# Four-head loads, the first batch's norm on VectorE, and v in token order in a Nystrom attention with two MLPs

## The chip, the core and the metric

The kernel runs on one core of a Trainium2 chip. The metric is the device time of one execution in microseconds (us); less is better. A NeuronCore has five engines that run side by side, each with its own instruction stream in a fixed order: TensorE (PE in the profile; its weight loads are PEld), VectorE (DVE), ScalarE (ACT), GpSimd (POOL) and SyncE (SP). Transfers between memory and the on-chip SBUF are issued by SP or ACT onto a queue and carried by 16 DMA engines.

## The reference

The input is q, k and v of 4 batches, 8 heads, 576 tokens and 64 channels. Per head the tokens are cut into 32 segments of 18, and a landmark is the mean of a segment. Then two MLPs run over the 2304 tokens of 512 channels.

```
q_lm, k_lm = segment means (32 landmarks of 18 tokens each)
A  = softmax(q  k_lm^T / 8)        # 576 x 32
Bm = softmax(q_lm k_lm^T / 8)      # 32 x 32
C  = softmax(q_lm k^T / 8)         # 32 x 576
Z  = Bm^T / (norm1 * norminf);  six times: Z = 2 Z - Z Bm Z
x  = A Z C v                       # heads side by side: 512 channels
x  = x / rms(x) * g;  x = (silu(x w_gate) * (x w_val)) w_out     # 512 -> 1536 -> 512
out = (s * relu(x w_in)^2 + b) w_out2                            # 512 -> 2048 -> 512
```

The MLP weights arrive as 64-bit floats and are narrowed to 32 bits on the chip.

## The kernel before

The kernel does not write its instructions down in the order in which they run. Every step is an entry in a list (`op`, and `at` inside `attention`) with the engines that may do it and an assumed duration on each, the buffers that it reads and writes, and a key. `Scheduler.run` plays the list through with those durations and emits an instruction when the planned clock reaches it, the smallest key first; so the order on every engine, and which engine does a step that has two, come from the plan. On the chip each engine then goes through its stream in that order and waits where a result is missing.

`attention(b, ...)` is one batch. Batches 2 and 3 are "fine" (`FINE = 2`), batches 0 and 1 are not; the change treats these two kinds differently. The steps of a batch: load q, k (two tiles each, `load_heads`, four heads of 32 landmarks on the 128 partitions of a tile) and v (`load_v`); sum the segments (`seg_sum`: in batch 0 a reduction on VectorE, in the others five adds per tile on GpSimd, L488 to L493); transpose q and k on TensorE (L528) with evictions on ScalarE (L532); the 32 x 32 scores Bm; the two halves of C (`c_side`: scores, maximum, exponential at L687, transposes at L704, product with v at L726); the four pieces of A (`a_side`); six Newton steps for Z (products at L586, updates at L631 on VectorE), after which `w_bd` (L790) forms Z C v; the product with A and its squares (L828, L834); the sum of squares over channels and the root (L848 to L859); a diagonal of the roots (L861), its product with ones on TensorE (L866) that spreads the root over partitions, the scaling (L872), and the split of x into two rounded parts (L876 and L878). That last part, from L834 on, is called the norm here.

The first MLP begins with `fused` (L993), which multiplies the norm's weights into w_gate and w_val, and `hidden`, whose matrix products stand at L1016 and whose element-wise steps at L1032 (tanh on ScalarE), L1034 and L1038. A batch has 12 such units of two halves, and `out_mm` follows. The first L1016 is where batch 0 of the MLP starts. The weights of the first MLP are loaded and narrowed while batch 0 runs: `narrow` loads 512 KB of 64-bit words into one of three `stage` buffers (L904 or L906, on SP) and needs four element-wise steps (L917 and L919 on ScalarE, L921 and L924 on VectorE, which reads two SBUF operands in both); the result is stored in device memory (L937, L949) and read again for batches 1 to 3. Where the plan leaves TensorE idle in the first 60 us, `warm` (L1248) puts products of ones there whose result nobody reads.

A load's order in time is its place in SP's stream; a load that must wait (for its buffer, or for the eighth DMA before it, since the DMAs share eight semaphores) holds all that stands behind it on SP.

Of the kernel before, what the change touches and what calls it, by code (L numbers as in the profile page):

```python
# [35 lines left out]
SCORE = 0.56  # L36
# [213 lines left out]
def tile_nystrom_attention_two_mlps(  # L250
# [150 lines left out]
    def attention(b, t0, t1):  # L401
# [17 lines left out]

        pair = xs[1, b] = (Buf(x_r[0]), Buf(x_r[1]))  # L420
# [130 lines left out]
        def b_mm(_):  # L551
            for g in range(2):
                if not fine:
                    for h in range(4):
                        p = slice(32 * h, 32 * h + 32)
                        nc.tensor.matmul(
                            out=pB.t[p, 32 * g:32 * g + 32], lhsT=bd["q", g].t[0:D, p],
                            rhs=bd["k", g].t[0:D, p], start=True, stop=True)
# [83 lines left out]
        def scores(ps, nm, g, hf, p0, r, w):  # L642
            d, t = bd["kq"[nm == "k"], g], tt[nm, g]
# [12 lines left out]
            def mm(_):  # L656
                for h in range(4):
                    p = slice(32 * h, 32 * h + 32)
                    e = slice(D * hf, D * hf + D)
                    nc.tensor.matmul(  # L660
                        out=ps.t[p, 0:HC], lhsT=d.t[e, p],
                        rhs=t.t[e].rearrange("p (t m) -> p t m", m=128)[:, :, p], start=True, stop=True)

            at(("pe", SCORE), p0 + 0.02, mm, r=[d, *[(t, i) for i in range(3)], *r], w=[ps, *w])
# [4 lines left out]
        def c_side(g, p0):  # L669
            transposed("k", g, p0)  # L670
# [15 lines left out]
            for hf in range(2):  # L686
                at(("act", t_act(HC) + 0.19), p0 + 0.03, lambda e, hf=hf: e.activation(  # L687
                    out=eC.t[:, HC * hf:HC * hf + HC], in_=pC[hf].t[:, 0:HC], func=ACTF.Exp,
                    scale=scale, bias=cm.t[:, 3:4], accum_out=cs.t[:, hf:hf + 1]),
                    r=[pC[hf], (cm, 3)], w=[(eC, hf), (cs, hf)])  # L690
# [19 lines left out]
            at(("pe", 0.13), p0 + 0.04, lambda e: tr(e, [4]), r=[(eC, 1), "ident", (pE[1], "taken")], w=[pE[1]])  # L710
# [29 lines left out]
        def a_side(hf, g, p0):  # L740
            if hf == 0:
                transposed("q", g, p0)
# [72 lines left out]
        for hf in range(2):  # L815
# [21 lines left out]
            if not first:  # L837
                for c, n in ((2, 2 * HC), (1, HC)):
                    at(dp(n), p0 + 0.03, lambda e, c=c, n=n, xq=xq: e.tensor_tensor(
                        out=xq.t[:, 0:n], in0=xq.t[:, 0:n], in1=xq.t[:, HC * c:HC * c + n], op=ALU.add),  # L840
                        r=[(xq, i) for i in range(KD)] if n > HC else [(xq, 0), (xq, c)],
                        w=[(xq, 0)] + ([(xq, 1)] if n > HC else []))
            n_sum = KD if first else 1
# [10 lines left out]
            def s_rec(e, pS=pS, rs=rs):  # L854
# [5 lines left out]
                out=rs.t[0:NP, 0:3], in_=rs.t[0:NP, 0:3], func=ACTF.Sqrt), r=[rs, "table"], w=[rs])  # L860
            at(dp(HC), p0 + 0.07, lambda e, rs=rs, dg=dg: e.tensor_tensor(  # L861
# [3 lines left out]
                op=ALU.mult), r=[rs, "ident"], w=[dg])  # L865
# [3 lines left out]
            for g in range(2):  # L869
# [8 lines left out]
                at(dp(HC), p0 + 0.1, lambda e, a=a, cols=cols: e.tensor_tensor(  # L878
                    out=part(1, "t")[:, cols], in0=a.t[:, 0:HC], in1=part(0, "t")[:, cols].bitcast(F32),
                    op=ALU.subtract), r=[a, wh[0]], w=wl)  # L880
# [103 lines left out]
    def fused(key, b, f):  # L984
# [12 lines left out]
        op(("pe", U_PE), key, mm, r=[gw[b], (r, 0), (r, 1)], w=[*pU, (uh, "taken"), (ul, "taken")])  # L997
# [287 lines left out]
```

## Time and profile before

| | |
|---|---|
| median of 3 runs | 906.83 us (901.38 to 908.39) |
| the profiled execution, its own time | 903.9 us |
| its span, first to last instruction | 902.2 us |
| TensorE busy | 870.2 us, 96% of the span |
| VectorE, ScalarE, GpSimd busy | 700.9, 430.0, 114.4 us |
| mean granted TensorE clock | 0.987 of full speed |
| moved by DMA | 105.99 MB, mean 117 GB/s |

The share of TensorE says little by itself: it holds the warm products of the first 60 us, and from 170 us on it is close to 99%. What differs between stages is what TensorE waits for, so the rows below are taken from stretches of the span.

### The profile page before, as it was taken

To read this page: it belongs to the slowest core of one execution; us is meant where nothing else is said; L and a number is where in the kernel's file an instruction comes from. 1 tells how busy PE (TensorE), PEld (TensorE's weight loads), DVE (VectorE), ACT (ScalarE), POOL (GpSimd) and SP (SyncE) were. 2 spreads that over 40 slices of the span, in tenths; PEclk is the share of its full clock that TensorE was granted. 3 is DMA by queue.
4 is the path that set the end of the run, shared out by engine and by line. 5 is a ranking of instruction groups with operands and counts; after the bars stand their busy time and mean duration, and the time that the engine had idled before them with its cause. 6 is when DMAs were issued, how large, how long until landed. Compare 5 with 4: busy or idle time off the path is not lost.

```text
span 902.2 us, 17055 instructions
## 1 busy us (share of the span) xinstructions
PE 870.2 (96%) x6453; PEld 726.4 (81%) x6453; DVE 700.9 (78%) x1486; ACT 430.0 (48%) x902; POOL 114.4 (13%) x152
## 2 busy tenths in 40 slices
PE   8897899899999999999999999999999999999997
PEld 5576666798788898899888988888888888888896
DVE  5768889889888889799889866676667666666686
ACT  3565566535465345555656533343343334333453
POOL 0442034500465004300000000000000000000000
PEclk9898999999999999999999999999999999999999
DMA  7778998886444432348887200010001000100100
GB/s 162 198 214 283 247 280 236 271 241 216 119 144 141 143 116 84 106 146 272 286 262 252 56 1 1 0 47 1 1 1 47 1 1 1 47 1 1 27 22 24
DMA packets 72899, 105.99 MB, mean 117 GB/s; under 512 B 25968, under 2 KB 46448, under 8 KB 72816
## 3 DMA queue, kind: packets, MB, share of 16 engines
q1 hardware_dynamic: 72240, 103.45, 38.3%
q10 hardware_dynamic: 576, 1.44, 0.7%
q8 instruction: 51, 0.84, 0.4%
q14 instruction: 32, 0.26, 0.1%
HBM read 90.70 MB, written 14.16 MB: 116 GB/s over the span
## 4 chain that ended last, share of the span: by engine, by line
PE 83%; DVE 8%; DMA 5%; ACT 2%; issue 1%; SPq 1%; ACTq 0%; DVEq 0%
PE bank L975 22%; PE bank L1091 22%; PE bank L1016 15%; PE bank L1065 12%; PE bank L1061 3%; PE bank L993 3%; DMA region<-in_q_dram 2%; DVE cmag L921 2%; DMA stage<-in_moe_w_out_dram 2%; PE bank L648 1%; PE bank L828 1%; DMA stage<-in_moe_w_gate_dram 1%; PE bank L1248 1%; DVE wl L893 1%; DVE rawg L924 1%
## 5 line engine op out<-in xcount | busy, mean ns | idle before, releaser
L1016 PE MATMUL bank<-xh,uh 128*128 128x288 f32 x384 | 124.2, 323 | 6.4 <-DVE hbuf L1034 3.1
L975 PE MATMUL bank<-xh,ul 128*128 128x512 f32 (+1 forms) x320 | 117.7, 368 | 0.0
L975 PE MATMUL bank<-xh,uh 128*128 128x512 f32 (+1 forms) x320 | 117.6, 368 | 0.0
L975 PE MATMUL bank<-xl,uh 128*128 128x512 f32 (+1 forms) x320 | 117.6, 368 | 0.0
L1016 PE MATMUL bank<-xl,uh 128*128 128x288 f32 x384 | 114.8, 299 | 0.0
L1016 PE MATMUL bank<-xh,ul 128*128 128x288 f32 x384 | 114.7, 299 | 0.0
L1091 PE MATMUL bank<-wh,hh 128*128 128x512 f32 x288 | 112.4, 390 | 0.3 <-DVE hh L892 0.3
L1091 PE MATMUL bank<-wl,hh 128*128 128x512 f32 x288 | 112.3, 390 | 0.0
L1226 ACT ACTIVATE hbuf<-bank 128x512 f32<-128x512 f32 (+1 forms) x79 | 43.9, 556 | 143.4 <-PE bank L975 143.3
L1091 PE MATMUL bank<-wh,hl 128*128 128x512 f32 x288 | 112.0, 389 | 0.0
L1016 PEld LDWEIGHTS bank<-xh,uh 128*128 128x128 f32 x384 | 73.6, 192 | 27.3 <-issue 5.0
L1065 PE MATMUL bank<-hh,wh 128*128 128x288 f32 x288 | 87.9, 305 | 1.1 <-ACT xbuf L1075 1.1
L1065 PE MATMUL bank<-hl,wh 128*128 128x288 f32 x288 | 84.9, 295 | 0.1
L1065 PE MATMUL bank<-hh,wl 128*128 128x288 f32 x288 | 84.6, 294 | 0.0
L893 DVE TENSOR_TENSOR hl<-hbuf,hh 128x512 fp32r<-128x512 f32 (+2 forms) x123 | 73.1, 595 | 2.3
L1016 PEld LDWEIGHTS bank<-xl,uh 128*128 128x128 f32 x384 | 73.7, 192 | 0.5
L1016 PEld LDWEIGHTS bank<-xh,ul 128*128 128x128 f32 x384 | 73.7, 192 | 0.0
L975 PEld LDWEIGHTS bank<-xh,uh 128*128 128x128 f32 x320 | 60.2, 188 | 11.1
L975 PEld LDWEIGHTS bank<-xl,uh 128*128 128x128 f32 x320 | 60.0, 188 | 10.9
L975 PEld LDWEIGHTS bank<-xh,ul 128*128 128x128 f32 x320 | 60.1, 188 | 10.2
L917 ACT ACTIVATE ca<-stage 128x512 f32<-128x512 f32 x68 | 45.9, 675 | 42.6 <-DMA stage<-in_moe_w_out_dram 12.0
L892 DVE CAST uh<-region 128x512 fp32r<-128x512 f32 x56 | 23.9, 426 | 54.4 <-PE bank L975 54.4
(193 smaller groups left out, 1822.9 us busy)
## 6 DMA issues: line engine op xcount, KB each, us to landing
rawo<-kepto SPq DMA_DIRECT2D x84, 256.0 KB, 3.3
rawg<-keptg SPq DMA_DIRECT2D x36, 512.0 KB, 3.9
stage<-in_moe_w_out_dram SPq DMA_DIRECT2D x28, 512.0 KB, 5.2
stage<-in_moe_w_in_dram SPq DMA_DIRECT2D x16, 512.0 KB, 4.6
stage<-in_moe_w_gate_dram SPq DMA_DIRECT2D x12, 512.0 KB, 5.3
stage<-in_moe_w_val_dram SPq DMA_DIRECT2D x12, 512.0 KB, 5.5
keptg<-rawg SPq DMA_DIRECT2D x12, 512.0 KB, 6.3
region<-in_k_dram SPq DMA_DIRECT2D x32, 144.0 KB, 5.3
```

Of the source, the lines that this page charges most:

```text
L648: nc.tensor.matmul(out=ps.t[:, 0:HC], lhsT=part(u, "bd")[:, 128 * e:128 * e + 128], rhs=part(y, "t").rearrange("p (t e i) -> p t e i", e=2 ...
L892: else e.tensor_copy(out=hi(), in_=src())), r=r, w=[wh], pair=True)
L893: b = op({"dve": t_dve(n), "pool": t_pool(n)}, key, lambda e: e.tensor_tensor(out=lo(), in0=src(), in1=hi().bitcast(F32), op=ALU.subtract) ...
L917: op(("act", 0.08 + t_act(512)), key, lambda e: e.activation(out=a.t, in_=word(1).bitcast(F32), func=ACTF.Copy, scale=2.0 ** -112), r=[st, ...
L921: op(("dve", t_dve(512)), key, lambda e: e.scalar_tensor_tensor(out=m.t, in0=word(1), scalar=-2 ** 31, in1=m.t, op0=ALU.bitwise_and, op1=A ...
L975: nc.tensor.matmul(out=ps.t[:, 0:n], lhsT=w[a].t[:, ks], rhs=x[y].t[:, kd, 0:n], start=(kd == 0 and i == 0), stop=(kd == KD - 1 and i == 2))
L993: nc.tensor.matmul(out=pU[g].t[m, 0:256], lhsT=gw[b].t[p, m], rhs=r.t[p, :, 128 * k:128 * k + 128], start=True, stop=True)
L1016: nc.tensor.matmul(out=ps.t[:, 0:HC], lhsT=u[a].t[:, 256 * g + 128 * part:256 * g + 128 * part + 128], rhs=x[y].t.rearrange("p k n -> p (k ...
L1061: nc.tensor.matmul(out=A[c].t[:, 0:HC], lhsT=r.t[:, 128 * c:128 * c + 128], rhs=h.t, start=(f == 0), stop=(f == F1 - 1))
L1065: nc.tensor.matmul(out=A[c].t[:, 0:HC], lhsT=w[a].t[:, 128 * c:128 * c + 128], rhs=hs[y].t[:, 0:HC], start=(f == 0 and i == 0), stop=(f == ...
L1091: nc.tensor.matmul(out=A[c].t, lhsT=hs[a].t[:, s], rhs=w[y].t, start=(f == 0 and i == 0), stop=(f == F2 - 1 and i == 2))
L1226: e.activation(out=r.t[:, 0:n], in_=ps.t[:, 0:n], func=ACTF.Relu) if e is nc.scalar
```

## The change

In batches 0 and 1 each tile of q and k comes with one DMA over 128 partitions (heads 4g to 4g+3) where four DMAs of 32 partitions each stood; all of them go to SP's queue, where batch 0's q was on ScalarE's before. As heads lie otherwise in the tiles now, `loaded(g, h)` says in which tile and rows head 2h+g is, and both tiles of a kind are transposed before the first scores. In all batches v comes with five DMAs, a token to a partition, where 18 of 32 partitions stood; the exponentials of C are written so that their columns are in token order too, 18 elements apart. In batch 0 the adds of the squares, the diagonal and the lower part of the split are given to VectorE alone (`near`), and the four squares per element are added on VectorE first, so that the column sums need 3 products where 12 stood (per half; 6 and 24 in all). The plan now counts these steps as using the port that VectorE and GpSimd share (`pair=True`). A tanh of one element after batch 0's roots loads that table earlier, and the first `fused` gets an earlier key.

```diff
@@ attention
+        def near(n):
+            return {"dve": t_dve(n)} if first else dp(n)
@@ load_heads
+                    if not fine:
+                        e.dma_start(
+                            out=t.t.rearrange("p (t d) -> p t d", d=D),
+                            in_=a[b, 4 * g:4 * g + 4].rearrange("h (i t) d -> (h i) t d", t=SEG))
+                        return
                     for h in range(4):
...
-                at(("act" if first and nm == "q" else "sp", 2.2 if first and nm == "q" else 5.2),
-                   -0.3 if b else 0, load_heads, w=[t])
+                at(("sp", 5.2 if fine else 3.64), -0.3 if b else 0, load_heads, w=[t])
@@ load_v
-            sv = v[b].rearrange("h (i n) d -> n i h d", n=SEG)
-            for n in range(SEG):
-                e.dma_start(out=vt()[32 * (n % 4):32 * (n % 4) + 32, n // 4], in_=sv[token(b, n)])
-
-        at(("sp", 9.5), -0.25 if b else 0.01, load_v, w=[vs])
+            for j in range(5):
+                n = min(128, S - 128 * j)
+                e.dma_start(out=vt()[0:n, j], in_=v[b, :, 128 * j:128 * j + n].rearrange("h s d -> s h d"))
+
+        at(("sp", 5.9), -0.25 if b else 0.01, load_v, w=[vs])
+        def loaded(g, h):
+            n = 2 * h + g
+            return n // 4, slice(32 * (n % 4), 32 * (n % 4) + 32)
@@ scores, b_mm: operands by loaded(g, h); the scores read both tiles
@@ c_side
-            transposed("k", g, p0)
+            for j in (g,) if fine else (0, 1) if g == 0 else ():
+                transposed("k", j, p0)
...
-                    out=eC.t[:, HC * hf:HC * hf + HC], in_=pC[hf].t[:, 0:HC], func=ACTF.Exp,
+                    out=(eC.t.rearrange("p (i n) -> p n i", n=SEG)[:, HB * hf:HB * hf + HB] if fine
+                         else eC.t.rearrange("p (i t f) -> p f t i", t=HB, f=2)[:, hf]),
+                    in_=pC[hf].t[:, 0:HC].rearrange("p (t i) -> p t i", i=32), func=ACTF.Exp,
@@ the norm
-            if not first:
-                for c, n in ((2, 2 * HC), (1, HC)):
-                    at(dp(n), p0 + 0.03, lambda e, c=c, n=n, xq=xq: e.tensor_tensor(
+            for c, n in ((2, 2 * HC), (1, HC)):
+                at(near(n), p0 + 0.03, lambda e, c=c, n=n, xq=xq: e.tensor_tensor(
...
-            n_sum = KD if first else 1
+            n_sum = 1
...
+            if first and hf:
+                at(("act", 1.4), 0.0, lambda e: e.activation(out=spare, in_=spare, func=ACTF.Tanh),
+                   r=[("root", 0, 0), ("root", 0, 1)], w=["spare"])
-            at(dp(HC), p0 + 0.07, lambda e, rs=rs, dg=dg: e.tensor_tensor(
+            at(near(HC), p0 + 0.07, lambda e, rs=rs, dg=dg: e.tensor_tensor(
...
-                at(dp(HC), p0 + 0.1, lambda e, a=a, cols=cols: e.tensor_tensor(
+                at(near(HC), p0 + 0.1, lambda e, a=a, cols=cols: e.tensor_tensor(
@@ fused
-        op(("pe", U_PE), key, mm, r=[gw[b], (r, 0), (r, 1)], w=[*pU, (uh, "taken"), (ul, "taken")])
+        op(("pe", U_PE), key - 12 if not (b or f) else key, mm, r=[gw[b], (r, 0), (r, 1)], w=[*pU, (uh, "taken"), (ul, "taken")])
```

The changed code has other line numbers; where both occur, L446 to L460 of before (loads of q, k and v) are L449 to L467, L488 to L493 are L501 to L506, L848 to L878 are L865 to L898, and L921, L924, L1016 are L941, L944, L1036.

Three places show what the plan makes of it. The first is SP's stream from its start to the fourth load of a weight into a stage buffer; before:

```order
L446 DMA region<-in_k_dram 32x1152 x8
L460 DMA region<-in_v_dram 32x8x64 x18
L906 DMA stage_91<-in_moe_w_gate_dram 128x4x128
L906 DMA stage_92<-in_moe_w_val_dram 128x4x128
L906 DMA stage_93<-in_moe_w_gate_dram 128x4x128
...
L446 DMA region<-in_k_dram 32x1152 x8
L446 DMA region<-in_q_dram 32x1152 x8
L906 DMA stage_91<-in_moe_w_val_dram 128x4x128
L906 DMA stage_92<-in_moe_w_gate_dram 128x4x128
L906 DMA stage_93<-in_moe_w_val_dram 128x4x128
L937 DMA keptg_114<-rawg_85 128x1024
L460 DMA region<-in_v_dram 32x8x64 x18
```

And now:

```order
L449 DMA region<-in_k_dram 128x1152 x2
L449 DMA region<-in_q_dram 128x1152 x2
L467 DMA region<-in_v_dram 128x8x64 x4
L467 DMA region<-in_v_dram 64x8x64
L926 DMA stage_91<-in_moe_w_gate_dram 128x4x128
...
L449 DMA region<-in_k_dram 128x1152 x2
L449 DMA region<-in_q_dram 128x1152 x2
L467 DMA region<-in_v_dram 128x8x64 x4
L467 DMA region<-in_v_dram 64x8x64
L926 DMA stage_91<-in_moe_w_val_dram 128x4x128
```

Nine DMAs stand ahead of the first weight load where 26 stood on SP and eight on ScalarE's queue, and batch 1's v, 18 DMAs between the sixth and the seventh weight load before, now stands with q and k ahead of the fourth.

The second place is VectorE from the mask of Z C v (L790, now L808) to the first scaling of the normalised x (L872, now L892); `cmag` and `rawg` are the two steps of narrowing a weight. Before, with buffer numbers:

```order
L790 TENSOR_TENSOR region_113<-bank0_63,mask2_74 128x128 x2
L798 TENSOR_TENSOR region_113<-region_113,mask1_75 128x256
L924 SCALAR_TENSOR_TENSOR rawg0_85<-ca1_95,cmag1_97 128x512
L921 SCALAR_TENSOR_TENSOR cmag0_96<-stage2_93,cmag0_96 128x512
L924 SCALAR_TENSOR_TENSOR rawg1_86<-ca0_94,cmag0_96 128x512
L855 TENSOR_SCALAR region_113<-bank2_65 96x3
...
L810 TENSOR_TENSOR gw0_106<-bank1_64,gT_77 128x128
...
L924 SCALAR_TENSOR_TENSOR rawg2_87<-ca1_95,cmag1_97 128x512
L872 TENSOR_TENSOR region_113<-region_113,bank3_66 128x288 x2
```

And now:

```order
L808 TENSOR_TENSOR region_113<-bank2_65,mask2_74 128x128 x2
L816 TENSOR_TENSOR region_113<-region_113,mask1_75 128x256
...
L856 TENSOR_TENSOR xbuf_80<-xbuf_80 128x576
L856 TENSOR_TENSOR xbuf_80<-xbuf_80 128x288
...
L881 TENSOR_TENSOR xbuf_80<-ident_71,region_113 96x288
...
L944 SCALAR_TENSOR_TENSOR rawg1_86<-ca1_95,cmag1_97 128x512
L881 TENSOR_TENSOR region_113<-ident_71,region_113 96x288
L892 TENSOR_TENSOR region_113<-region_113,bank1_64 128x288 x2
L941 SCALAR_TENSOR_TENSOR cmag0_96<-stage1_92,cmag0_96 128x512
L898 TENSOR_TENSOR xl0_83<-region_113,xh0_81 128x288 x2
```

The adds, the diagonals and the lower parts of the split stand on VectorE among the narrowing steps now, and five narrowing steps fewer stand ahead of the first scaling.

The third place is GpSimd after batch 0's last product of A (L767, now L785). Before:

```order
L767 TENSOR_TENSOR xbuf_80<-xbuf_80,region_113 128x288
L488 TENSOR_TENSOR region_113<-region_113 128x576
L491 TENSOR_TENSOR region_113<-region_113 128x256
...
L488 TENSOR_TENSOR region_113<-region_113 128x576
L861 TENSOR_TENSOR xbuf_80<-ident_71,region_113 96x288
L861 TENSOR_TENSOR region_113<-ident_71,region_113 96x288
L878 TENSOR_TENSOR xl0_83<-region_113,xh0_81 128x288 x4
L491 TENSOR_TENSOR region_113<-region_113 128x256
```

And now:

```order
L785 TENSOR_TENSOR xbuf_80<-xbuf_80,region_113 128x288
L501 TENSOR_TENSOR region_113<-region_113 128x576
L504 TENSOR_TENSOR region_113<-region_113 128x256
...
L506 TENSOR_TENSOR region_113<-region_113 128x64
L501 TENSOR_TENSOR region_113<-region_113 128x576
L504 TENSOR_TENSOR region_113<-region_113 128x256
```

The segment sums of batch 1's four tiles follow each other without batch 0's norm between them.

## Rows read from the trace of the kernel before

**Rows 1.** Stretches: length, busy us by engine, granted clock, DMA share, GB/s.

```profile
61.00:78.00 17.00, 13.99 (x128) 12.04 (x127) 14.53 (x28) 11.45 (x23) 11.71 (x16) 0.90 0.87 285
...
170.00:477.00 307.00, 303.12 (x2907) 265.23 (x2906) 268.59 (x621) 158.82 (x368) 60.98 (x80) 1.00 0.57 179
...
477.00:516.00 39.00, 37.59 (x226) 33.54 (x225) 34.43 (x68) 22.69 (x45) 0.00 (x0) 1.00 0.47 149
...
516.00:902.00 386.00, 381.52 (x1772) 318.75 (x1770) 263.77 (x474) 151.33 (x269) 0.00 (x0) 1.00 0.05 13
...
70.00:80.00 10.00, 9.74 (x74) 9.07 (x75) 9.39 (x19) 5.92 (x13) 3.41 (x5) 0.83 0.89 285
```

**Rows 2.** The same view, stretches of 2 us with loads in flight.

```profile
6.00:8.00 2.00, 0.11 (x2) 0.00 (x0) 0.00 (x0) 0.00 (x0) 0.00 (x0) 1.00 1.00 205
16.00:18.00 2.00, 2.00 (x22) 1.36 (x22) 2.00 (x2) 1.86 (x6) 0.00 (x0) 1.00 0.57 130
24.00:26.00 2.00, 0.33 (x16) 0.22 (x16) 1.83 (x11) 0.85 (x2) 0.00 (x0) 0.98 1.08 373
26.00:28.00 2.00, 1.32 (x40) 1.09 (x40) 1.76 (x8) 2.00 (x7) 0.38 (x1) 0.50 0.97 226
```

**Rows 3.** DMA issues, from the page: count, KB, us to landing.

```profile
rawg<-keptg SPq DMA_DIRECT2D x36, 512.0 KB, 3.9
```

**Rows 4.** Timeline to 33 us: start, us, engine, line, what, idle before.

```profile
8.71 2.12 DVE L474 TENSOR_REDUCE region<-region 128x64 f32<-128x1152 f32 x1 [7.13 <-DMA region<-in_k_dram]
...
10.09 10.51 SPq L460 DMA_DIRECT2D region<-in_v_dram  x18
...
13.62 6.30 DVE L474 TENSOR_REDUCE region<-region 128x64 f32<-128x1152 f32 x3 [2.78 <-DMA region<-in_k_dram]
...
25.15 0.66 ACT L917 ACTIVATE ca<-stage 128x512 f32<-128x512 f32 x1 [2.57 <-DMA stage<-in_moe_w_gate_dram]
...
32.23 0.29 DVE L631 SCALAR_TENSOR_TENSOR region<-region,bank 128x128 f32<-128x128 f32 x1 [4.33 <-issue]
```

**Rows 5.** Timeline from w_bd to the first product of the MLP.

```profile
43.25 0.47 DVE L790 TENSOR_TENSOR region<-bank,mask 128x128 f32<-128x128 f32 x2
...
45.72 4.26 PE L848 MATMUL bank<-ones,xbuf 128*96 128x1 f32 x48
...
47.64 11.07 SPq L460 DMA_DIRECT2D region<-in_v_dram  x18
...
52.84 4.16 PE L1248 MATMUL bank<-ones 128*128 128x256 bf16 x35
...
58.81 0.40 SPq L906 DMA_DIRECT2D stage<-in_moe_w_gate_dram  x1
...
60.79 0.38 PE L1016 MATMUL bank<-xh,uh 128*128 128x288 f32 x1
...
60.97 1.28 ACT L1032 ACT_TABLE_LOAD   x1
```

**Rows 6.** Timeline, GpSimd's segment sums and VectorE's narrowing at 62 to 69 us.

```profile
62.18 1.67 POOL L491 TENSOR_TENSOR region<-region 128x256 f32<-128x256 f32 x3
...
64.33 1.43 POOL L488 TENSOR_TENSOR region<-region 128x576 f32<-128x576 f32 x1
...
65.83 2.32 POOL L491 TENSOR_TENSOR region<-region 128x256 f32<-128x256 f32 x3
...
65.89 1.22 DVE L921 SCALAR_TENSOR_TENSOR cmag<-stage,cmag 128x512 int32<-128x512 int32 x1
...
68.24 0.68 DVE L921 SCALAR_TENSOR_TENSOR cmag<-stage,cmag 128x512 int32<-128x512 int32 x1
```

**Rows 7.** One line's instructions: times in ns, minimum, median, maximum.

```profile
L839 DVE TENSOR_TENSOR region<-region x6: 749/755/1396, 149.3 to 367.1; 128x576 f32<-128x576 f32 x6
```

**Rows 8.** Timeline after 70 us: TensorE's longest wait, and batch 2's v.

```profile
70.06 0.43 PE L1016 MATMUL bank<-xh,uh 128*128 128x288 f32 x1 [2.81 <-DVE hbuf L1034]
...
138.50 9.72 SPq L460 DMA_DIRECT2D region<-in_v_dram  x14
```

More of the change, by code (lines that the diff above doesn't have):

```diff
@@ L554, in b_mm @@
                     for h in range(4):
-                        p = slice(32 * h, 32 * h + 32)
+                        i, p = loaded(g, h)
                         nc.tensor.matmul(
-                            out=pB.t[p, 32 * g:32 * g + 32], lhsT=bd["q", g].t[0:D, p],
-                            rhs=bd["k", g].t[0:D, p], start=True, stop=True)
+                            out=pB.t[32 * h:32 * h + 32, 32 * g:32 * g + 32], lhsT=bd["q", i].t[0:D, p],
+                            rhs=bd["k", i].t[0:D, p], start=True, stop=True)
                     continue
@@ L642, in scores @@
         def scores(ps, nm, g, hf, p0, r, w):
[L643 removed]
+            other = "kq"[nm == "k"]
             if fine:
@@ L657, in mm @@
                 for h in range(4):
-                    p = slice(32 * h, 32 * h + 32)
+                    i, p = loaded(g, h)
                     e = slice(D * hf, D * hf + D)
                     nc.tensor.matmul(
-                        out=ps.t[p, 0:HC], lhsT=d.t[e, p],
-                        rhs=t.t[e].rearrange("p (t m) -> p t m", m=128)[:, :, p], start=True, stop=True)
-            at(("pe", SCORE), p0 + 0.02, mm, r=[d, *[(t, i) for i in range(3)], *r], w=[ps, *w])
+                        out=ps.t[32 * h:32 * h + 32, 0:HC], lhsT=bd[other, i].t[e, p],
+                        rhs=tt[nm, i].t[e].rearrange("p (t m) -> p t m", m=128)[:, :, p], start=True, stop=True)
+            at(("pe", SCORE), p0 + 0.02, mm, r=[*[bd[other, j] for j in range(2)],
+                *[(tt[nm, j], i) for j in range(2) for i in range(3)], *r], w=[ps, *w])
         Cv = Buf(cv_r)
         def c_side(g, p0):
-            transposed("k", g, p0)
+            for j in (g,) if fine else (0, 1) if g == 0 else ():
+                transposed("k", j, p0)
             pC = [Buf(ps_r), Buf(ps_r)]
@@ L741, in a_side @@
             if hf == 0:
-                transposed("q", g, p0)
+                for j in (g,) if fine else (0, 1) if g == 0 else ():
+                    transposed("q", j, p0)
             pA, A, a = Buf(ps_r), Buf(a_ring), Buf(AT_r)
@@ L836, in attention @@
             pS, pR, rs, dg = Buf(ps_r), Buf(ps_r), Buf(sm_r), Buf(a_ring)
-            if not first:
-                for c, n in ((2, 2 * HC), (1, HC)):
-                    at(dp(n), p0 + 0.03, lambda e, c=c, n=n, xq=xq: e.tensor_tensor(
-                        out=xq.t[:, 0:n], in0=xq.t[:, 0:n], in1=xq.t[:, HC * c:HC * c + n], op=ALU.add),
-                        r=[(xq, i) for i in range(KD)] if n > HC else [(xq, 0), (xq, c)],
-                        w=[(xq, 0)] + ([(xq, 1)] if n > HC else []))
-            n_sum = KD if first else 1
+            for c, n in ((2, 2 * HC), (1, HC)):
+                at(near(n), p0 + 0.03, lambda e, c=c, n=n, xq=xq: e.tensor_tensor(
+                    out=xq.t[:, 0:n], in0=xq.t[:, 0:n], in1=xq.t[:, HC * c:HC * c + n], op=ALU.add),
+                    r=[(xq, i) for i in range(KD)] if n > HC else [(xq, 0), (xq, c)],
+                    w=[(xq, 0)] + ([(xq, 1)] if n > HC else []), pair=True)
+            n_sum = 1
             def s_mm(_, pS=pS, xq=xq):
```

10 lines of the change are left out of this document (5 added, 5 removed).

## The prediction

> **What bounds the kernel now.** First the stretches of the span [rows 1]. From 170 us to the end TensorE is busy for 303.12 of 307, 37.59 of 39 and 381.52 of 386 us: nothing in the change touches those products, so that part is only moved, earlier or later, by what happens before it. From 61 to 78 us it is busy for 13.99 of 17 and VectorE for 14.53: there the MLP of batch 0 runs while its weights are loaded and narrowed. Before 61 us no product of the MLP has run at all. The time to win or lose therefore lies ahead of 170 us, and the larger part of it ahead of 60.79, where the first L1016 stands [rows 5].
>
> Then the timeline to 33 us [rows 4]. VectorE waits 7.13 us for k, sums a tile in 2.12 us, waits again for 2.78 and sums the other three in 6.30; it ends at 19.92. Behind that the chain goes through ScalarE, which stands for 2.57 us at the first weight because its load is queued behind the 18 DMAs of v (10.09 to 20.60), and VectorE stands for 4.33 us before the first Newton update at 32.23. The Newton steps end at 43.25 with w_bd. From there to the first L1016 are 17.5 us [rows 5]: column sums of 4.26 us (48 records), roots, and 35 warm products (4.16 us) that TensorE's order puts ahead of the spreading of the roots.
>
> **The loads of q and k.** The stretches of 2 us [rows 2] show what a transfer to 32 partitions costs: at 6 to 8 us, with nothing but these loads, the DMA engines are full (share 1.00) and move 205 GB/s, at 26 to 28 us 226. At 24 to 26 us, with weights that go to 128 partitions, they move 373 at the same share. I take 373 for the new loads, 205 as the other end. One tile is 576 KB (590 thousand bytes). The nearest transfer of that shape, 512 KB to 128 partitions, lands 3.9 us after its issue [rows 3]; the first issue stays at 0.8 us, so the first tile is there at 0.8 + 3.9 + 0.2 = 4.9 us and the others 1.6 us apart, at 6.5, 8.1 and 9.7. None is waited for then: four sums of 2.1 us end at 13.3 where they ended at 19.92. At 205 GB/s the last of 2.36 MB lands near 13.9 and the sums end at 16.0; if the first comes a microsecond sooner, at 12.3. Gain 6.6 us, bounds 3.9 and 7.6.
>
> The Trainium skill (SBUF — State Buffer, "Door 1: the DMA port swizzle") says that DMA bandwidth depends on how many of 16 SBUF ports the partitions reach, and by its table 32 consecutive partitions reach eight. The trace agrees, with 205 to 226 against 373 GB/s; by the rule alone the lower bound of the gain would go.
>
> **From the sums to w_bd.** The first weight stands behind q, k and v now. The last tile of q lands at 9.7; v's pieces moved at 130 GB/s for a share of 0.57 [rows 2], 228 at a full share, so 5.2 us for 1.18 MB; with the weight's own 1.4 us it lands at 16.3 instead of 25.15. ScalarE comes to it about 2 us after the sums, at 15.3, so its 2.57 us shrink to one. The first Newton product stood behind the second half of the transposed exponentials on TensorE and now stands ahead of it, so VectorE's 4.33 us can go; but VectorE's order brings a transpose, a row sum and six small steps forward that stood behind the first update, some 1.7 us. I take a gain of 1.5, bounds 0 and 2.6. The Newton stretch itself, 11.0 us, loses those 1.7 and gets one narrowing step more ahead of w_bd, 0.68 us alone and 1.9 at worst: 0, bounds -0.5 and 0.7. The exponentials written 18 elements apart have no row of their own. The sums read 1152 elements 64 apart in 2.12 us, 1.84 ns each [rows 4], the add of 576 neighbours takes 0.755 us, 1.31 ns each [rows 7]; a third more of the two exponentials on the path would be 0.3 us, inside these bounds.
>
> **From w_bd to the MLP.** With the squares added first, a quarter of the column sums is left: 4.26 us become 1.1. What VectorE has to do in its new order up to the first pair of lower parts: w_bd 0.47 [rows 5], five narrowing steps of 0.68 [rows 6], adds of 0.755 [rows 7] and 0.4 for either half, two diagonals, two scalings and two lower parts of 0.4 each, and some 1.5 of small steps, estimated: 10.1 us. TensorE's order has 32 warm products behind the second spreading, at 4.16/35 each 3.8 us; they start at about 8.5 us, so the first product of the MLP comes at 13 us and not at 17.5. That is one end. The other is GpSimd. Its segment sums for batch 1 now follow one another without a break, 1.43 + 1.67 us and a short last add per tile [rows 6], beside exactly this work. Where both ran before, at 65.8 us, three adds took 2.32 us and not 1.67 and the narrowing step 1.22 and not 0.68 [rows 6]; an add of VectorE's took 1.396 once and not 0.755 [rows 7]. Four tiles are some 13.5 us; about 5.5 of them fit ahead of w_bd, where the GpSimd of before did one tile and the first add of the next. The other 8 fall behind it; if VectorE waits out each, its 10.1 become 18. I take 15.5, a gain of 2, bounds -0.5 and 4.5, since not every step of VectorE meets one of GpSimd.
>
> **After the first product of the MLP.** The tanh table, 1.28 us at 60.97 [rows 5], is loaded earlier, beside the norm. The sums that GpSimd has done by then no longer meet VectorE. Batch 1's v held SP for 11.07 us, and the seventh weight was issued at 58.81 behind it [rows 5]; TensorE's wait of 2.81 us at 70.06 for a step that stands behind narrowing [rows 8] has its root there, and batch 2's v held SP for 9.72 again. Five DMAs need some 2.5 us. Against that, five narrowing steps fewer are done when the first product of the MLP runs, of which the earlier starts give back all but about two, 1.4 us. I take a gain of 2, bounds -1 and 5. From 170 us on nothing changes.
>
> **The sum.** 6.6 + 1.5 + 0 + 2 + 2 = 12.1 us. Against the profiled execution, 903.9 - 12.1 = 891.8; that execution is 2.9 us under the median of the runs, well inside their spread, so I say 892. All lower bounds together leave 1.9 us (902), all upper ones 20 (884).
>
> **The rivals.** (a) *The gain of the norm goes to the shared port and the exponentials, and q and k come at the old rate.* For it: [rows 6]. Gain 4 to 8 us, 896 to 900. Half of this is that VectorE waits out all of GpSimd's sums, which alone makes 12.1 into 9.6, 894.3. The Trainium skill (SBUF — State Buffer, "SBUF: two separate sides") calls the port pair of the two an exclusive lock, held for a whole instruction; the trace shows steps 0.5 us longer there [rows 6], less than a whole add of 1.4. (b) *The weights set the pace of the first twelve units*, so that the earlier start is waited off at the first units: VectorE's 14.53 of 17 us [rows 1] speak for it; against it, that the weight loads move forward as well, the fourth to sixth by as much as the Newton steps do. Gain 2 to 5, 899 to 902. (c) *Slower: TensorE's clock.* In 70 to 80 us it was granted 0.83 on the mean [rows 1], partly at 1.2 GHz, after the wait at 70.06. If the first units come 12 us sooner but the weights do not, the gaps are longer and the lower level lasts; each microsecond at 1.2 GHz gives back half of one. It turns the sum over from 24 us at that level and makes the kernel slower by over 1% from 42 us, which is 913. Nothing in [rows 1] comes near that. (d) *More*: the two holds of SP were worth all 5 us and the port nothing: 884 to 888.
>
> **How the numbers follow.** Forecast (gain 9 to 15) 0.55, (a) 0.22, (b) 0.08, (c) 0.06, (d) 0.09. The range of 885 to 902 takes in the forecast, (a), (b) and half of (d). One per cent, about what a measurement of this kernel can tell from no change, is 9 us: faster by more is the forecast, (d) and the top of (a), 0.70; within it the rest of (a) and (b), 0.23; slower 0.07.
>
> **What would show it.** In the profile after: four sums of segments back to back, ending at 13 us; share 1.0 at about 370 GB/s up to 8 us; no wait of ScalarE over 1 us at the first weight; w_bd near 35, the first product of the MLP near 51; no hold of SP over 4 us at batch 2's v. I am wrong if the sums still wait for q or k, if VectorE's steps behind w_bd are each as long as GpSimd's adds beside them, or if TensorE waits for more than 10 us in its first 60 us of MLP work.

## The result, and the profile after

The changed kernel takes 895.39 us (median of 9 runs, 891.53 to 898.85) where the kernel before takes 906.04: a ratio of 0.9893, interval 0.9867 to 0.9918, so 10.6 us faster. The two profiled executions differ by less, 902.2 and 895.2 us of span; readings of the trace below have these 7.0 us to explain.

First the stretches of the span, to set beside [rows 1] and [rows 2].

```profile
2.00:4.00 2.00, 2.00 (x11) 1.45 (x10) 0.00 (x0) 0.08 (x1) 0.00 (x0) 1.00 0.96 309
4.00:6.00 2.00, 2.00 (x11) 1.71 (x10) 1.47 (x1) 0.39 (x1) 0.00 (x0) 1.00 1.03 417
6.00:8.00 2.00, 1.80 (x16) 1.38 (x16) 2.00 (x2) 1.58 (x5) 0.00 (x0) 1.00 1.01 408
...
61.00:78.00 17.00, 15.01 (x147) 12.12 (x146) 14.99 (x32) 11.39 (x27) 0.00 (x0) 1.00 0.94 295
170.00:477.00 307.00, 303.40 (x2895) 265.80 (x2893) 269.03 (x624) 165.61 (x379) 62.92 (x79) 1.00 0.58 181
...
516.00:895.00 379.00, 374.57 (x1741) 313.11 (x1739) 257.43 (x462) 146.46 (x260) 0.00 (x0) 1.00 0.05 13
```

At a full share the loads now move 408 to 417 GB/s where they moved 205. From 61 to 78 us GpSimd no longer works (11.71 us before), the granted clock is 1.00 and not 0.90, and TensorE is busy a microsecond longer. From 170 us on TensorE is as busy as before. The clock of 61 to 78 us is not a gain of the whole, though: it falls again, to 0.83 in 80 to 90, 100 to 110 and 140 to 150 us, and over 60 to 120 and 120 to 180 us it is what it was before, 0.94 and 0.97 (the lines of before stand under "Which hold of SP"). TensorE alone:

```profile
60.00:120.00 60.00, 53.10 (x526) 0.94 0.86 269
120.00:180.00 60.00, 56.02 (x521) 0.97 0.87 260
```

Then the timeline of the changed kernel, the rows that answer to [rows 4], [rows 5], [rows 6] and [rows 8]:

```profile
2.67 8.18 SPq L467 DMA_DIRECT2D region<-in_v_dram  x5
...
4.53 8.33 DVE L487 TENSOR_REDUCE region<-region 128x64 f32<-128x1152 f32 x4 [2.95 <-DMA region<-in_k_dram]
...
15.99 0.66 ACT L937 ACTIVATE ca<-stage 128x512 f32<-128x512 f32 x1 [0.77 <-DMA stage<-in_moe_w_gate_dram]
...
26.16 0.29 DVE L644 SCALAR_TENSOR_TENSOR region<-region,bank 128x128 f32<-128x128 f32 x1 [2.60 <-PE bank L599]
...
28.74 5.37 SPq L467 DMA_DIRECT2D region<-in_v_dram  x5
...
36.35 0.47 DVE L808 TENSOR_TENSOR region<-bank,mask 128x128 f32<-128x128 f32 x2
...
37.08 1.47 POOL L501 TENSOR_TENSOR region<-region 128x576 f32<-128x576 f32 x1
...
37.21 1.89 DVE L941 SCALAR_TENSOR_TENSOR cmag<-stage,cmag 128x512 int32<-128x512 int32 x1
...
51.68 0.47 ACT L545 ACTIVATE region<-bank 128x384 f32<-128x384 f32 x1
...
52.20 6.10 PE L1268 MATMUL bank<-ones 128*128 128x256 bf16 x32 [3.54 <-ACT region L545]
...
58.14 0.49 PE L541 MATMUL bank<-ident,region 128*128 128x128 f32 x3
...
58.38 0.38 PE L1036 MATMUL bank<-xh,uh 128*128 128x288 f32 x1
...
130.02 6.42 SPq L467 DMA_DIRECT2D region<-in_v_dram  x5
```

The four sums run without a break and end at 12.86, 7.06 us earlier than before. w_bd comes 6.9 us earlier (36.35 for 43.25). The first hidden product comes only 2.4 us earlier (58.38 for 60.79): the stretch between the two grew from 17.5 to 22.0 us. So 4.6 of the 7.0 us were won after the first product of the MLP.

### The profile page after: what moved, and what is told of

Its sections match the earlier page's. It is cut to its first block, busy times and chain, and to the rows that moved or that the text cites. A ratio compares the mean times of both kernels' runs of the same rounds, so it can differ in the third digit from the quotient of the medians.

```text
span 895.2 us, 16809 instructions
## 1 busy us (share of the span) xinstructions
PE 863.5 (96%) x6381; PEld 720.7 (81%) x6381; DVE 701.3 (78%) x1493; ACT 436.0 (49%) x908; POOL 111.4 (12%) x144
## 4 chain that ended last, share of the span: by engine, by line
PE 81%; DVE 11%; DMA 3%; ACT 2%; issue 2%; SPq 1%; DVEq 0%; ACTq 0%
PE bank L995 22%; PE bank L1111 22%; PE bank L1036 14%; PE bank L1085 12%; PE bank L1081 3%; PE bank L1013 2%; DVE cmag L941 1%; DMA stage<-in_moe_w_gate_dram 1%; PE bank L1268 1%; PE bank L661 1%; DVE wl L913 1%; SPq L467 1%; DMA rawo<-kepto 1%; DMA stage<-in_moe_w_val_dram 1%; PE bank L599 1%
## 5 line engine op out<-in xcount | busy, mean ns | idle before, releaser
L1036 PE MATMUL bank<-xh,uh 128*128 128x288 f32 x384 | 123.9, 323 | 4.7 <-DVE ul L1024 2.4
L1036 PE MATMUL bank<-xh,ul 128*128 128x288 f32 x384 | 114.2, 297 | 0.0
L1036 PE MATMUL bank<-xl,uh 128*128 128x288 f32 x384 | 114.0, 297 | 0.0
L1246 ACT ACTIVATE hbuf<-bank 128x512 f32<-128x512 f32 (+1 forms) x79 | 43.9, 555 | 143.4 <-PE bank L995 143.3
L1036 PEld LDWEIGHTS bank<-xh,uh 128*128 128x128 f32 x384 | 73.1, 190 | 24.7 <-issue 4.0
L1085 PE MATMUL bank<-hh,wh 128*128 128x288 f32 x288 | 87.5, 304 | 1.2 <-ACT xbuf L1095 1.2
L1085 PE MATMUL bank<-hl,wh 128*128 128x288 f32 x288 | 84.9, 295 | 0.3 <-DVE hl L913 0.3
L1085 PE MATMUL bank<-hh,wl 128*128 128x288 f32 x288 | 84.7, 294 | 0.4 <-DVE wl L913 0.4
L1036 PEld LDWEIGHTS bank<-xl,uh 128*128 128x128 f32 x384 | 73.1, 190 | 0.7
L1036 PEld LDWEIGHTS bank<-xh,ul 128*128 128x128 f32 x384 | 73.0, 190 | 0.2 <-DVE ul L1024 0.2
```

The lines of the kernel that those rows point to most:

```text
L1036: nc.tensor.matmul(out=ps.t[:, 0:HC], lhsT=u[a].t[:, 256 * g + 128 * part:256 * g + 128 * part + 128], rhs=x[y].t.rearrange("p k n -> p (k ...
L1085: nc.tensor.matmul(out=A[c].t[:, 0:HC], lhsT=w[a].t[:, 128 * c:128 * c + 128], rhs=hs[y].t[:, 0:HC], start=(f == 0 and i == 0), stop=(f == ...
L1246: e.activation(out=r.t[:, 0:n], in_=ps.t[:, 0:n], func=ACTF.Relu) if e is nc.scalar
```

## The experiments

Twelve kernels, each timed in five rounds against the kernel before; ratios are to that kernel, measured on the same chip. The diffs below show the main lines only; what belongs to a part in the change above (operands, the plan's durations) came with it.

| kernel | median us | ratio | interval |
|---|---|---|---|
| loads of q and k alone | 895.96 | 0.9882 | 0.9859 to 0.9905 |
| v alone | 897.42 | 0.9904 | 0.9880 to 0.9928 |
| norm alone | 903.81 | 0.9975 | 0.9958 to 0.9991 |
| loads and v, old norm | 893.48 | 0.9864 | 0.9842 to 0.9886 |
| v in batch 1 alone | 897.01 | 0.9888 | 0.9869 to 0.9907 |
| v in batches 2 and 3 alone | 901.28 | 0.9946 | 0.9928 to 0.9965 |
| changed, sums held by the order | 897.72 | 0.9898 | 0.9880 to 0.9917 |
| changed, 46 warm products out | 888.07 | 0.9806 | 0.9785 to 0.9827 |
| changed, only 32 of them out | 892.37 | 0.9867 | 0.9840 to 0.9894 |
| changed, 46 out, sums really held | 892.39 | 0.9866 | 0.9844 to 0.9887 |
| loads and v, old norm, 54 warm out | 895.99 | 0.9890 | 0.9872 to 0.9907 |
| before, 74 warm products out | 903.49 | 0.9979 | 0.9962 to 0.9996 |

### Which part of the change it is

Theory L says that the gain is the earlier start, S that it is SP, no longer held by v, N that it is the norm and GpSimd's absence from the first units. The loads alone, on the kernel before:

```diff
-                    for h in range(4):
-                        e.dma_start(out=t.t[32 * h:32 * h + 32]..., in_=a[b, 2 * h + g]...)
+                    if not fine:
+                        e.dma_start(out=t.t..., in_=a[b, 4 * g:4 * g + 4]...)
+                        return
```

> The kernel before with the four-head loads of q and k alone (v by 18 DMAs, batch 0's norm as before). Theory L, that the gain is the earlier start: VectorE's four sums end near 13 us instead of 19.92 and most of that is carried to the end, 5 to 8 us faster than before, so 898 to 901. Theory S, that the gain of 10 us is mostly SP, which v no longer holds in batches 1 and 2: only 1 to 3 us faster, 903 to 905, because v's 18 DMAs still stand ahead of the weights at the start and hold SP twice later. Theory N, that it is GpSimd's work and the norm in the first units of the MLP: also 1 to 3 us.

v alone:

```diff
-            for n in range(SEG):
-                e.dma_start(out=vt()[32 * (n % 4):..., n // 4], in_=sv[token(b, n)])
+            for j in range(5):
+                e.dma_start(out=vt()[0:n, j], in_=v[b, :, 128 * j:128 * j + n]...)
-                    out=eC.t[:, HC * hf:HC * hf + HC], ... func=ACTF.Exp,
+                    out=eC.t.rearrange("p (i t f) -> p f t i", t=HB, f=2)[:, hf], ... func=ACTF.Exp,
```

> The kernel before with v loaded in token order by five DMAs and the exponentials written to token order, and nothing else. Theory S: batch 1's and batch 2's holds of SP, 11.07 and 9.72 us before, shrink to under 5.5, and the kernel is 3 to 6 us faster, 900 to 903. Theories L and N: within 2 us of before, 904 to 908, since the sums still end near 20 us; the exponentials written strided, 0.79 us and not 0.49 in the changed kernel, cost up to 0.6 of it.

The norm alone:

```diff
-            n_sum = KD if first else 1
+            n_sum = 1
-            at(dp(HC), p0 + 0.1, ...
+            at(near(HC), p0 + 0.1, ...
```

> The kernel before with batch 0's norm alone changed: squares added first, adds, diagonals and lower parts on VectorE, tanh table loaded early, the first fused product 12 earlier in the order. Theory N: 4 to 7 us faster, 899 to 902, since GpSimd is clear of the first units of the MLP. Theories L and S: between 2 us slower and 2 us faster, 904 to 908, since in the changed kernel the stretch from w_bd to the first hidden product grew from 17.5 to 22 us with this norm.

All but the norm:

```diff
-                at(near(HC), p0 + 0.1, ...
+                at(dp(HC), p0 + 0.1, ...
```

> The changed kernel without the new norm: loads of q and k and of v as changed, batch 0's norm as before. Theories L and S together: 8 to 11 us faster than before, 895 to 898, as the changed kernel or a little better, because its stretch from w_bd to the first hidden product lost 4 us. Theory N: less than half of the gain is left, 901 to 904.

The loads alone make 10.2 us, more than any theory said, and v alone 8.8, together 12.7, so they win the same thing in part twice; the norm makes 2.4 alone and, on top of the other two, nothing (0.9864 without it, 0.9893 with it, intervals that overlap). v alone is the surprise, for its sums still end at 19.81 us and its first hidden product stands at 60.18: it wins 0.6 us ahead of the MLP. That is S and more than S expected.

All but the norm came out faster than expected, and not for the reason given: its stretch from w_bd to the first hidden product is no shorter than 22.0 us but longer, 26.6 (35.19 to 61.81), with 39 warm products just ahead of that product. It comes 3.4 us later than in the changed kernel, and the kernel is no slower: TensorE then goes on without a gap (about 1 of the 17.00 us in the last line is the end of the warm products).

```profile
54.90 7.15 PE L1261 MATMUL bank<-ones 128*128 128x256 bf16 x39 [3.21 <-ACT region L540]
61.81 0.38 PE L1029 MATMUL bank<-xh,uh 128*128 128x288 f32 x1
...
61.00:78.00 17.00, 17.00 (x170) 1.00 0.68 215
```

So when the first hidden product starts does not settle the time by itself. In the timeline of the loads alone, batch 1's v, still 18 DMAs, has moved:

```profile
27.61 10.32 SPq L464 DMA_DIRECT2D region<-in_v_dram  x18
...
51.01 0.38 PE L1027 MATMUL bank<-xh,uh 128*128 128x288 f32 x1
...
53.15 0.38 SPq L917 DMA_DIRECT2D stage<-in_moe_w_gate_dram  x1
```

Its hold of SP ends at 37.9 instead of 58.71 [rows 5], and the seventh weight is issued at 53.15 instead of 58.81. The loads alone therefore change the start and the hold at once and can't tell L from S.

### Which hold of SP

v in token order for one batch at a time leaves the start alone. Batch 1 only, and batches 2 and 3 only:

```diff
+            if not (b == 1):        # the other kernel: b >= 2
                 for n in range(SEG):
                     e.dma_start(out=vt()[32 * (n % 4):..., n // 4], in_=sv[token(b, n)])
+                return
+            for j in range(5): ...
```

> The kernel before with v by five DMAs (and exponentials to token order) in batch 1 alone. v alone in all batches made 8.8 us, with no gain before the first hidden product. Theory H, that every hold of SP by v costs the MLP beside it some microseconds: batch 1's hold (47.64 to 58.71 before) becomes some 6 us and earlier, TensorE's wait of 2.8 us at 70 us and the clock under 1.00 behind it go, 3 to 5 us faster, 901 to 903. Rival B, that the gain starts in batch 0, where the first weight stood behind v: within 1.5 us of before.

> The kernel before with v by five DMAs in batches 2 and 3 alone. Theory H: the holds of 11.83 us at 136 and 10.45 at 239 shrink to 5 to 7, the waits of TensorE between 140 and 180 us (3.5 us and a clock of 0.91 in 160 to 180) go, 3 to 5 us faster, 901 to 903, and with the run of batch 1 alone it adds up to the 8.8. Rival B: within 1.5 us of before.

Batch 1 alone gives 9.8 us, as much as v in all batches; batches 2 and 3 give 5.5, though batch 2's hold shrank to 8.63 us only (batch 3's to 4.84). Rival B is out, and a shorter hold pays in either place, the first at twice the price of theory H; but the two add up to 15.3 and not, as H said, to the 8.8. One rival is not tested: each edit also tells the plan that v takes 5.9 us and not 9.5, and the plan then orders every engine anew. The timeline of batch 1 alone:

```profile
46.20 6.33 SPq L465 DMA_DIRECT2D region<-in_v_dram  x5
52.63 0.66 SPq L914 DMA_DIRECT2D stage<-in_moe_w_gate_dram  x1
...
55.77 0.37 SPq L914 DMA_DIRECT2D stage<-in_moe_w_gate_dram  x1
...
69.78 0.40 PE L1024 MATMUL bank<-xh,uh 128*128 128x288 f32 x1 [0.90 <-DVE hbuf L1042]
```

The seventh and ninth weight come 6.2 and 4.1 us earlier than before, and TensorE's wait at 70 us is 0.90 and not 2.81 [rows 8]. It does not wait less in all there: waits of 1.13 and 1.17 us at 64.50 and 75.54 have come in, and from 61 to 78 us it is busy for 13.80 us where it was for 13.99 [rows 1], but at a clock of 1.00 and not 0.90:

```profile
61.00:78.00 17.00, 13.80 (x135) 1.00 0.67 199
```

What that does to the MLP shows in stretches of 60 us, TensorE's busy time, clock, DMA share and GB/s, first of the kernel before:

```profile
60.00:120.00 60.00, 50.95 (x496) 0.94 0.90 273
120.00:180.00 60.00, 55.54 (x530) 0.97 0.84 255
```

and of v in batch 1 alone:

```profile
60.00:120.00 60.00, 52.31 (x537) 1.00 0.87 270
120.00:180.00 60.00, 56.61 (x543) 1.00 0.84 252
```

Busy time times clock is 47.9 and 52.3 us in the first stretch, 53.9 and 56.6 in the second: 7.2 us more work done by 180 us, where the spans differ by 7.5 (902.2 and 894.7). Some 4.8 of the 7.2 are the clock, which here stays at 1.00 from 60 us on; 2.3 are busy time, 0.8 of it warm products. The products themselves give a little less: the last hidden one of the first MLP starts at 474.4 us for 480.1, 5.7 us earlier, and the rest of the 7.5 is won behind it, where TensorE was busy for 37.59 of 39 us before [rows 1] and is now for 39.00. No load of v stands there; for that part the plan's other order is a likelier cause than the hold, and neither is shown.

### From w_bd to the first hidden product

Three causes were possible for the 22.0 us: GpSimd's sums beside the norm (P), the 32 warm products (W), or neither, because VectorE sets the pace of the MLP anyway (V).

```diff
-  ... op=ALU.add), r=[s3], w=[tmp, (lm, "taken")])
+  ... op=ALU.add), r=[s3, *([("a", g) for g in range(2)] if b == 1 else [])], w=[tmp, (lm, "taken")])
```

> The changed kernel with GpSimd's segment sums of batch 1 waiting for batch 0's lower parts, so that VectorE does the norm with GpSimd idle. Theory P, that these sums lengthen VectorE's norm: w_bd to the first hidden product is 22.0 us in the changed kernel and falls to 16 to 18, the steps of L941 beside it to 0.7 from 1.1 to 1.9, and the kernel is 2 to 4 us faster than the changed one, 892 to 894. Rival V, that VectorE and the narrowing set the pace up to 170 us whenever the first product comes: the stretch shortens as well, but the time is within 2 us of the changed kernel, or slower by up to 3, because the sums now run beside the MLP.

This one answers nothing on P: the reads added are marks that only the plan sees, so it put the sums later, but on GpSimd nothing stood in front of them and no result was missing, so they ran when they did in the changed kernel (31.92 there). It shows that such an edit of the order is worth nothing by itself (0.9898 for 0.9893):

```profile
31.49 1.95 POOL L501 TENSOR_TENSOR region<-region 128x576 f32<-128x576 f32 x1
```

```diff
-WARM1 = 60.0
+WARM1 = 35.0
```

> The changed kernel with the 32 warm products (6.10 us at 52.20) taken out that stand ahead of the first hidden product, and 14 later ones. Theory W, that they delay the first product: it comes near 53 us and not at 58.4, and the kernel is 2 to 5 us faster than the changed one, 890 to 893. Rival V: the first product comes earlier, but the narrowing of the next weights does not, within 1.5 us of the changed kernel. Rival C, the clock: the first products run at 1.2 GHz, and the granted clock of 50 to 80 us falls; 1 to 4 us slower, 896 to 899.

The first hidden product comes at 52.69 us, as W said, and the time falls by more than it said: 888.07 us, the fastest kernel of this study, 18.7 us under the kernel before and, by the two ratios, 7.9 under the changed one. Its timeline, where TensorE waits as long for ScalarE as in the changed kernel, and then goes straight on:

```profile
51.87 0.90 PE L541 MATMUL bank<-ident,region 128*128 128x128 f32 x3 [3.54 <-ACT region L545]
52.69 0.61 PE L1036 MATMUL bank<-xh,uh 128*128 128x288 f32 x1
```

Its stretches of 2 us (TensorE's busy time, clock, DMA):

```profile
52.00:54.00 2.00, 2.00 (x8) 0.50 0.14 30
54.00:56.00 2.00, 2.00 (x25) 0.67 0.96 251
56.00:58.00 2.00, 2.00 (x29) 1.00 0.94 246
```

and those of the changed kernel:

```profile
54.00:56.00 2.00, 2.00 (x12) 0.50 0.00 0
56.00:58.00 2.00, 2.00 (x14) 0.69 0.00 0
```

Rival C has it the wrong way round in this kernel: the clock was at 1.2 GHz in both (0.50 in 48 to 52 us, where TensorE had 0.46 and 0.66 us of work), and without the warm products it is back at 1.00 two microseconds sooner, with real products. With only the 32 out:

```diff
-                    warm()
+                    warm() if t <= SKIP[0] or t > SKIP[1] else None
```

> The changed kernel with the 32 warm products ahead of the first hidden product taken out, the 14 later ones left in. Theory W: these 32 are the whole of the 8 us, 887 to 890. Rival: the later 14 hold part of it (2.0 us of TensorE's time at 65.89, 70.29 and 76.79), 890 to 892.

its first hidden product comes at 51.98 us, but the time falls to 892.37 only, 2.4 us under the changed kernel by the ratios, with intervals that overlap. So that the 32 delay the first product is shown, and what they cost in time is not. The 14 later ones take about 2 us of TensorE and seem to be worth some 5 (0.9806 for 0.9867). They do not cost it where they stand: counted over the products of L1036, L1081 and L1085, the 281st starts at 132.3 us here and at 133.5 with all 46 out, the 301st at 143.3 and 140.5. Between them lies a wait of TensorE for batch 1's squares, first here, then with all 46 out:

```profile
139.08 0.40 PE L1036 MATMUL bank<-xh,uh 128*128 128x288 f32 x1 [4.16 <-ACT region L852]
...
137.86 0.41 PE L1036 MATMUL bank<-xh,uh 128*128 128x288 f32 x1 [1.72 <-ACT region L852]
```

Why it differs stays open.

Then GpSimd held for good, by a copy that needs the norm's last result, with the 46 out:

```diff
+        if b == 1:
+            at(("pool", 0.1), 0.0, lambda e: e.tensor_copy(out=spare2, in_=xs[1, 0][1]...[:, 3 * HC:3 * HC + 1]),
+                r=[(xs[1, 0][1], ("a", 1, 1))], w=["held"])
```

> The changed kernel without the 46 warm products and with a one-element copy on GpSimd, ahead of batch 1's segment sums, that reads the last lower part of batch 0: now GpSimd really is idle during the norm (in the run of the sums held by the order alone it was not: its sums ran from 31.5 to 50.7 us as in the changed kernel). Theory P: the narrowing steps beside the norm fall from 1.1 to 1.9 us to 0.7, w_bd to the first hidden product from 16.7 us to 12 to 14, but the sums then run beside the first units, as before the change; time 886 to 889, within 2 us of the run without the 46. Rival Q, that the sums cost as much in the MLP as in the norm or more, and batch 1's scores come later: 2 to 6 us slower than that run, 890 to 894.

```profile
40.36 0.68 DVE L946 SCALAR_TENSOR_TENSOR cmag<-stage,cmag 128x512 int32<-128x512 int32 x1
...
46.83 0.18 POOL L444 COPY spare<-xl 128x1 f32<-128x1 f32 x1 [15.47 <-DVE xl L903]
46.97 1.42 POOL L506 TENSOR_TENSOR region<-region 128x576 f32<-128x576 f32 x1
...
47.16 0.61 PE L1041 MATMUL bank<-xh,uh 128*128 128x288 f32 x1
...
47.35 1.58 DVE L946 SCALAR_TENSOR_TENSOR cmag<-stage,cmag 128x512 int32<-128x512 int32 x1
```

P is right on the stretch: the narrowing step is 0.68 us with GpSimd idle and 1.58 as soon as its add runs beside it, and w_bd to the first product takes 12.6 us (34.55 to 47.16) where it took 16.7. Q is right on the time: 892.39, some 5 us slower than with the sums beside the norm. But the price is not paid where the sums now run, from 46.97 to 65.5 us: counted as above, the first product is 5.5 us ahead of the run without the 46, the 241st still 7.5 (111.7 for 119.2), and the lead is lost between there and the 461st (176.4 for 174.5). That batch 1's scores come later, as Q says, would fit; it is not shown.

### What the norm is worth

```diff
 (loads and v, old norm)
-WARM1 = 60.0
+WARM1 = 35.0
```

> Loads of q, k and v as changed, batch 0's norm as before, and the 54 warm products from the norm on taken out (11 ahead of the first spreading, 39 ahead of the first hidden product). Theory N, that the new norm is worth something once the warm products are gone: 890 to 893, 2 to 5 us slower than the changed kernel without them. Rival O, that it never was: within 1.5 us of it, 887 to 889, or faster.

895.99 us, 0.9890 against 0.9806 with the new norm: with the warm products gone, the norm's change is worth 7.6 us. Its own warm products, on the other hand, cost this kernel nothing: with them it had 0.9864, with intervals that overlap. The timeline shows GpSimd doing norm and sums in the first units, and what TensorE waits for there:

```profile
50.32 0.61 PE L1029 MATMUL bank<-xh,uh 128*128 128x288 f32 x1
...
55.72 1.98 POOL L499 TENSOR_TENSOR region<-region 128x256 f32<-128x256 f32 x3
...
60.62 0.61 PE L1029 MATMUL bank<-xh,uh 128*128 128x288 f32 x1 [4.89 <-DVE hbuf L1047]
```

Its first product is 2.4 us earlier than that of the kernel with the new norm, and is followed by a wait of 4.89 us for VectorE. About that wait the clock is at 1.2 GHz and stays low behind it:

```profile
50.00:60.00 10.00, 5.34 (x29) 3.20 (x28) 5.98 (x9) 6.08 (x12) 8.05 (x10) 0.50 0.89 306
60.00:70.00 10.00, 9.38 (x74) 8.58 (x80) 8.55 (x18) 4.85 (x12) 5.08 (x9) 0.77 0.73 207
```

With the new norm and no warm products it is back at 1.00 by 56 us. The mean clock of all executions is 0.981 here, 0.986 there and 0.989 with this kernel's warm products in, so a part of the 7.6 us goes with the clock, which rival C had feared for the changed kernel. Last, the kernel before without its warm products from the norm on:

```diff
-WARM1 = 60.0
+WARM1 = 35.0
```

> The kernel before without the 35 and 15 warm products that stand among batch 0's norm and the 24 after them. The 46 taken out of the changed kernel made it 8 us faster. Theory D, that warm products are dear only where the chain of the norm waits for them: before, the 35 (4.16 us at 52.84) stand ahead of the spreading of the roots, so 2 to 5 us faster than before, 902 to 905. Rival A, that they cost the same wherever they are: 8 us faster, 898. Rival C, the clock: without them the products of the norm and the first hidden ones run at 1.2 GHz, and the time is 0 to 3 us longer.

903.49 us, ratio 0.9979: 2 us. Its first product comes 3.5 us earlier (57.27), but from 61 to 78 us the clock is 0.82, where it was 0.90 [rows 1]:

```profile
61.00:78.00 17.00, 13.58 (x113) 0.82 0.85 275
```

So A is out, and D's range holds at its lower end, but C had its part: the mean clock of the 12 executions is 0.982, that of the kernel before beside them 0.985. Warm products from 35 us of the plan on thus cost 7.9 us in the changed kernel, 2 in the kernel before and nothing with loads and v alone. That this depends on what waits behind it, as D says, is argued; the runs don't separate it from the clock that the filler kept up.

## Why the prediction came out, and where its steps failed

The time (892 forecast, 895.39 measured) lies inside the range and near the forecast, but two of the five terms have the wrong sign, and one makes up for a part of them. That it lies so near is in part luck: between the two profiled executions, 903.9 and 896.89 us, the gain is 7.0 of the 12.1 forecast. The 10.6 of the medians has 3.6 more, since the kernel before was profiled in an execution faster than its median and the changed one in a slower one; which stage they belong to is not known.

- *The loads, 6.6 forecast.* 7.06 in the profile; the rate, 408 to 417 GB/s, is above the 373 taken.
- *Sums to the first Newton update, 1.5 forecast.* It lost 1.0 (13.3 us for 12.3). ScalarE's wait at the first weight fell to 0.77 as said. But VectorE still waits 2.60 us at the first update: TensorE has the transposed exponentials, eight warm products and C's 40 products with v ahead of that Newton product. The strided exponentials were under-priced (next section), which is small here: sums to w_bd is 22.25 us with loads and v and 21.87 with the loads alone.
- *The Newton stretch, 0 forecast.* It gained 0.8, a little past its bound of 0.7.
- *w_bd to the first hidden product, 2 forecast.* It lost 4.5, past the lower bound of -0.5; this step failed. The experiments take it apart: 12.6 us with GpSimd held and no warm products, 4.1 more for GpSimd's sums (16.7), 5.4 more with the warm products (22.0). The first two are what the prediction weighed, 13 to 18. The third it put beside VectorE's work, 3.8 us at full clock from 8.5 us on. In the trace they start only 15.9 us behind w_bd, at 52.20, when the last lower part was nearly done: after the second spreading TensorE waited 3.54 us for ScalarE's eviction of a transpose (L545 at 51.68), which stood behind batch 0's upper parts in ScalarE's order, and after that wait the 32 ran at 1.2 GHz and took 6.10. Another transpose (58.14) and the first hidden product stand behind them. What the lost 4.5 us cost at the end is another matter: with loads and v alone the stretch is 26.6 us and the kernel no slower.
- *After the first product, 2 forecast.* 4.6 in the profile, inside its bounds of -1 to 5. The cause named, the two holds of SP, was under-priced as far as it can be tested by itself: batch 1's alone is worth 9.8 us when nothing else is changed. One wait of 2.81 us was seen [rows 8]; the clock that falls behind it and the later weights were not counted. In the changed kernel the clock is not what won the 4.6, for over 60 to 180 us it is as low as before; what did is not taken apart.

Of the rivals, (a) is right on the port, at 4.1 us nearer to its 5 than to the 2.5 in the forecast, and wrong on the rate. (b), that the weights set the pace, is right in the sense that weights held back on SP decide more than the first product does. (c) did not come, though the clock was at 1.2 GHz ahead of the MLP, from 48 to about 57 us. (d) is right that the holds were worth more than their price and wrong that the port was free. Of the signs named, the sums, the rate, the first weight and w_bd (36.35 for 35) came; the first product near 51 did not, nor a hold under 4 us at batch 2's v (6.42): five DMAs were taken at 2.5 us, and their issue took 5.37 to 8.18. Of the signs of being wrong none came in full: the sums wait for k only at the start, the step at 37.21 is longer than the add beside it (1.89 and 1.47) but not every one is, and in its first 60 us of MLP work TensorE is idle for 6.9 us.

So the total was near partly because errors cancelled. Loads and v without the norm would have been as good (0.9864), and the same change without the warm products after 35 us of the plan is 7.9 us better. What is not settled: why the later 14 warm products are worth 5 us, how much of the loads' own 7 us is carried to the end (the loads add 4 us to v, with intervals that overlap a little), and how much of each difference of a few us is the plan's other order, which every edit brings with it.

## What to carry to other kernels

When a change moves a whole start-up forward, look at what the order has put there as filler: products that were free while a chain was late can stand in its way when it is early. Then measure it, for such filler cost 7.9 us in one kernel here and nothing in another. Price a queue's hold by all the loads behind it and by the clock that falls with the wait they cause, not by the one wait that the trace names. And before a step is moved off an engine that shares a port, ask beside what it will then run: GpSimd's sums cost the norm 4 us, and the kernel that held them until the norm was done was 5 us slower all the same.

## What the hardware showed unexpectedly

The exponential of 128x288 takes 0.79 us when it writes 72 bytes apart, and 0.50 when it writes neighbours; the lines before and after the change, in ns (minimum, median, maximum):

```profile
L687 ACT ACTIVATE region<-bank,region x14: 484/498/513, 21.1 to 339.0; 128x288 f32<-128x288 f32 x14
...
L702 ACT ACTIVATE region<-bank,region x14: 782/793/813, 19.3 to 332.6; 128x288 f32<-128x288 f32 x14
```

That is 1.6 times as long, where a third more was estimated. The Trainium skill (SBUF — State Buffer, "Specifications (TRN2)") says that each step to a new 16-byte line of SBUF pays a penalty; the trace agrees in direction.

Five DMAs of 256-byte pieces hold SP's queue for 5.37 to 8.18 us in the changed kernel, 1.1 to 1.6 each on the mean, where the 18 of before took 0.58 each (10.51): fewer DMAs were not proportionally shorter to issue.

Beside a GpSimd add of 1.47 us at 37.08 the narrowing step at 37.21 took 1.89 and not 0.68: 1.21 us more, where 1.34 of the add were left. At 31.92 it was the other way round: an add took 1.96 us, and the step that began at 31.93 took 0.67. The Trainium skill (SBUF — State Buffer, "SBUF: two separate sides") calls the port pair an exclusive lock under which the loser blocks; by these rows it does, more fully than the 0.5 us that the prediction read from [rows 6].
